# Attention accumulators laid out by head and query half in a four-layer attention kernel

## The chip, the cores and the metric

The kernel runs on one core of a Trainium2 chip. The metric is the device time of one execution in microseconds. The kernel before takes 5525.5 us (median of 3 runs, 5524.3 to 5525.83).

## The reference

Four layers follow one another on x of shape [1, 2048, 576]. Layers 0 and 2 are multi-head attention (32 heads of 18 channels, with keys and values of their own), layers 1 and 3 have one key and one value head for all 32 query heads. Everything is float32.

```python
x = x + _A_ref(_layernorm(x), A_wqkv, A_wo)
x = x + _B_ref(_layernorm(x), B_wq, B_wk, B_wv, B_wo)
x = x + _A_ref(_layernorm(x), A_wqkv, A_wo)
x = x + _B_ref(_layernorm(x), B_wq, B_wk, B_wv, B_wo)
# within a layer, per head:
scores = jnp.einsum("bhqd,bhkd->bhqk", q, k) * (Dh ** -0.5)
p = softmax(scores); o = jnp.einsum("bhqk,bhkd->bhqd", p, v)
```

## The kernel before, in words

A layer projects queries, keys and values, and then goes through 16 pairs of heads (index p), each in four quarters of 512 queries (index u). There are 64 such blocks a layer and 256 in all. For one block (p, u) three kinds of work run on TensorE (PE).

- Row maxima: 32 matmuls of 128 queries by 512 keys (`max_mm`, lines 639 and 653), each read by VectorE (DVE, lines 656 and 658), some of them first copied by ScalarE (ACT, line 651). They run 14 steps (`LEAD`) ahead of the exponentials.
- Scores and exponentials: 32 matmuls of 128 keys by 512 queries (`exp_mm`, line 879), each followed by one ACT instruction (line 883), which writes a tile `pt` of 128 x 512. Tile i belongs to head a = (i // 2) % 2 of the pair and to key chunk kc = i // 4 * 2 + i % 2, so that each head has 16 chunks of 128 keys.
- Values: `pv_block` (line 921) multiplies `pt` by the values with a column of ones beside them, 19 columns, into the PSUM bank `oacc`. A float32 matmul appears in the trace as two instructions and two weight loads.

`oacc` has four groups of 32 partitions. Before the change group j = 64a + 32(kc % 2) holds head a, summed over the even or over the odd key chunks, for all 512 queries. One block of `pv_block` takes two key chunks and both heads, that is four tiles `pt`, one in each group; the four groups run at the same time in four column strips of the array.

The order of the work on PE is written out by hand. `UNIT` is a list of ten units; each names its 4 to 7 score and maximum matmuls (called rows here), and how many columns of values follow them: 448, 480, 320, 256, 480, 448, 416, 416, 416, 416. Ten units make 4096 columns, which is one block (eight steps of 512). Values lag by `PV_LAG` = 928 columns, the first two units. `pv_cols` cuts a unit's columns at the borders of the accumulator's width, and each piece is four matmuls of one width. Rows take their PSUM bank from seven in turn, the oldest first, so a row waits until ACT or DVE has read what was there.

After a block's last piece, one instruction copies `oacc` away to a tile `oc`: ACT (line 930) while maxima are still to be done, otherwise DVE (two blocks a layer). GpSimd (POOL) then adds the two halves of the keys (`o_sum`: two copies and one addition into `sums[u % 2]`). The rest of the way goes through DRAM and is run by `run_todo` at due times counted in steps from the block's end: `l_part` (5) loads the row of sums of exponentials, `l_inv` (8) takes the reciprocal on POOL, `l_out` (8) and `l_rows` (11) store it and load it again spread over partitions into `rb`, `o_mul` (13) multiplies on POOL, and `o_out` (15) stores the result to `o_d`. All DMAs are issued by SyncE (SP) in program order, among them `max_rows`, which brings the maxima to the scores' operand two steps before they are used. `sums` has two buffers, one for even and one for odd quarters.

Of the kernel before, what the change touches and what calls it, by code (L numbers as in the profile page):

```python
# [8 lines left out]
F32 = mybir.dt.float32  # L9
F32R = mybir.dt.float32r  # L10
AF = mybir.ActivationFunctionType
OP = mybir.AluOpType
# [5 lines left out]
DH = D // H  # L18
P = 128
NCH = S // P  # L20
# [25 lines left out]
STEPS = 8  # L46
LEAD = 14
NM_AT = 2.5
ROW_AT = 5
SUM_AT = 3.75  # L50
L_AT = 5
INV_AT = 8
R_AT = 8
RB_AT = 11
# [32 lines left out]
def tile_kernel(ctx: ExitStack, tc: tile.TileContext, A_x, A_wqkv, A_wo, B_x, B_wq, B_wk, B_wv, B_wo, out):  # L87
    nc = tc.nc
# [3 lines left out]
    cst = ctx.enter_context(tc.tile_pool(name="cst", bufs=1))  # L92
# [32 lines left out]
    oacc = psum.tile([P, 512], F32, name="oacc")  # L125
# [16 lines left out]
    o_d = dram.tile([D, S], F32, name="o_d")  # L142
    r_d = dram.tile([H, S], F32, name="r_d")
    x_d = dram.tile([len(AWAY), P, D], F32, name="x_d")

    rb = cst.tile([P, 512], F32, name="rb")

    sums = [cst.tile([P, 512], F32, name=f"os{i}") for i in range(2)]

# [29 lines left out]
    def ptile(name, shape=(P, 512), dt=F32):  # L179
        return pool.tile(list(shape), dt, tag="p", bufs=15, name=name)  # L180

    def copy(eng, dst, src):
        if eng is nc.scalar:
            eng.activation(dst, src, AF.Copy)
        else:
            eng.tensor_scalar(dst, src, 1.0, 0.0, op0=OP.mult, op1=OP.add)  # L186
# [271 lines left out]
    for layer in range(4):  # L458
        is_a = layer % 2 == 0
# [6 lines left out]
        def v_of(c):  # L466
            return vs[c // 8][:, c % 8] if is_a else vs[0][:, c]
# [73 lines left out]
        def q_slot(p):  # L541
            return (3, 5, 1)[p % 3] if is_a else (3, 4, 0)[p % 3]
# [38 lines left out]
                    fixed_rows(k_slot(p), True)  # L581
                load_rows(k_slot(p), D + 2 * p * DH, DH, 0, S, (i - 2,))

        mxs, nms, pts, ocs = {}, {}, {}, {}

        def ops(p):
            return big[:, q_slot(p)], big[:, k_slot(p)]
# [11 lines left out]
        for a in range(2):  # L599
            n = -4 * LEAD % 32  # L600
# [6 lines left out]
            left = [(i // 2 % 4, i // 8 * 2 + i % 2) for i in range(16)]  # L607
            left = [x for x in left if x not in order]
# [11 lines left out]
        ns = STEPS * 4 * NPAIR  # L620
# [281 lines left out]
        turn, pv_at = [0], [0]  # L902

        def pv_cols(cols):

            while cols:
                n, c0 = divmod(pv_at[0], 512)
                w = min(cols, 512 - c0)
                pv_block(n, c0, c0 + w)
                pv_at[0] += w  # L910
                cols -= w

        def pv_block(n, c0, c1):

            p, u, i = *divmod(n // STEPS, 4), n % STEPS * 4
            cs = slice(c0, c1)
            turn[0] += 1
            for i in range(i, i + 4) if turn[0] % 2 else range(i + 3, i - 1, -1):
                a, kc = (i // 2) % 2, i // 4 * 2 + i % 2
                j = 64 * a + 32 * (kc % 2)  # L920
                nc.tensor.matmul(oacc[j:j + DH + 1, cs], v_of(kc)[:, 2 * p + a if is_a else 0, :], pts[p, u, i][:, cs],  # L921
                                 start=kc < 2 and c0 == 0, stop=kc >= 14 and c1 == 512)
                if c1 == 512:
                    pt = pts.pop((p, u, i))
                    free.extend(j for j, x in enumerate(ring) if x is pt)
            if c1 == 512 and i // 4 == STEPS - 1:
                oc = ocs[p, u] = ocs["tile"]
                ticks[0] += 1
                if m_done[0] < 4 * ns:
                    nc.scalar.activation(oc, oacc, AF.Copy)  # L930
                else:
                    copy(nc.vector, oc, oacc)


        def o_sum(p, u):
            oc = ocs.pop((p, u))
            t = sums[u % 2]
            for j in (0, 64):
                copy(nc.gpsimd, t[j:j + 32], oc[j + 32:j + 64])
            nc.gpsimd.tensor_tensor(t[:96], t[:96], oc[:96], op=OP.add)  # L940

        def l_part(p, u):
            lt = lts[p, u] = pool.tile([P, 8], F32, name="lt")
            for a in range(2):
                nc.sync.dma_start(lt[64 * a:64 * a + 64, :], sums[u % 2][64 * a + DH:64 * a + DH + 1, :])

        def l_inv(p, u):
            rl = rls[p, u] = pool.tile([P, 8], F32, name="rl")
# [5 lines left out]

        def l_rows(p, u):
            for a in range(2):
                nc.sync.dma_start(rb[64 * a:64 * a + DH, :],
                                  r_d[2 * p + a:2 * p + a + 1, u * 512:(u + 1) * 512].to_broadcast([DH, 512]))

        def o_mul(p, u):  # L960
            t = sums[u % 2]
            nc.gpsimd.tensor_tensor(t[:96], t[:96], rb[:96], op=OP.mult)  # L962

        def o_out(p, u):
            for a in range(2):
                c = (2 * p + a) * DH
                nc.sync.dma_start(o_d[c:c + DH, u * 512:(u + 1) * 512], sums[u % 2][64 * a:64 * a + DH, :])


        relu, raw = (pool.tile([P, 640], F32, tag="xh", bufs=2, name=n) for n in ("relu", "raw"))  # L970
# [3 lines left out]
        def at(b, f, *args):  # L974
            todo.setdefault(b, []).append((f, args))
# [12 lines left out]
        for p in range(NPAIR):  # L988
            for u in range(4):
                b = STEPS * (4 * p + u) + STEPS - 1  # L990
                if is_a or p or u:
                    at(b + NM_AT, max_store, p, u)
                    at(b + (SOON[2] if b == ns - 1 else ROW_AT), max_rows, p, u)
                soon = p == NPAIR - 1 and u == 0
                for d, f in ((SUM_AT, o_sum), (L_AT, l_part), (INV_AT, l_inv), (R_AT, l_out), (RB_AT, l_rows),
                             (SOON[0] if soon else MUL_AT, o_mul), (SOON[1] if soon else O_AT, o_out)):
                    at(b + LEAD + d, f, p, u)
            if p + 1 < NPAIR and is_a:
                for d, f in ((0, diff_in), (3, diff_split), (5, diff_out), (10 if p else 8, diff_rows)):
                    at(max(LEAD, 32 * p - 8) + d, f, p + 1)  # L1000
            if is_a and p in (0, 1):
                at(LEAD + 20 + 32 * p, load_rows, q_slot(p + 1), 2 * (p + 1) * DH, DH, 1536, S)
            if p + 1 < NPAIR:
                for i in range(4 if is_a else 2):
                    at(LEAD + 32 * (p - 1) + 1 + 8 * i if p else LEAD + 1 + 4 * i, load_part, p + 1, i)
# [12 lines left out]
        def run_todo(st):  # L1018
            for n in sorted(n for n in todo if n <= st):
                for f, args in todo.pop(n):  # L1020
                    f(*args)
# [11 lines left out]
            f(*args)  # L1033
        assert not weave["left"] and m_done[0] == 4 * LEAD
        e_next = [0, 0]
        ocs["tile"] = ptile("oc")

        def exp_next(a, rank=0):
            pu, kc = divmod(e_next[a], NCH)
            exp_mm(*divmod(pu, 4), kc // 2 * 4 + 2 * a + kc % 2, rank)  # L1040
            e_next[a] += 1

        phase = lagged = 0
        while m_done[0] < 4 * ns:
            rows, cols = UNIT[phase % len(UNIT)]
            run_todo(LEAD + sum(e_next) / 4)
            for kind, a, rank in rows:
                if kind == "e":
                    exp_next(a, rank)
                elif m_done[0] < 4 * ns:  # L1050
                    max_mm(oldest(rank))
            skip = min(cols, PV_LAG - lagged)
            lagged += skip
            pv_cols(cols - skip)
            phase += 1
# [4 lines left out]
        while sum(e_next) < 4 * ns:  # L1060
            run_todo(LEAD + sum(e_next) / 4)
            for _ in range(min(4, 4 * ns - sum(e_next))):
                exp_next(int(e_next[0] > e_next[1]), next(i for i, j in enumerate(lru) if j not in held))
            left, c = 4 * ns - sum(e_next), -pv_at[0] % (512 * STEPS)
            if left < 4 * STEPS and 0 < c <= 512:
                pv_cols(c)
                for _ in range(FIRST[0]):
                    next(first)
                pv_cols(512 - c)
            else:  # L1070
                if left // 4 == 1:
                    for _ in range(FIRST[1]):
                        next(first)
                pv_cols(512)
# [39 lines left out]
```

## Time and profile before

| | kernel before |
|---|---|
| median time | 5525.5 us |
| profiled execution, span | 5520.9 us (4.6 us below the median time) |
| PE busy | 5509.2 us (100%) |
| DVE busy | 4920.3 us (89%) |
| ACT busy | 4889.3 us (89%) |
| POOL busy | 1839.9 us (33%) |
| chain that ended last | PE 97%, of it line 921 38%, line 879 27%, line 653 17% |

Busy times of PE overlap, since matmuls in different strips of the array run together, and their ends are modelled; so PE's pace is read from the distance between starts and not from its busy share. The span has four stretches of about 1.1 ms in which the blocks follow one another, one for each layer, with projections between them.

### The profile page before, as it was taken

The numbers are of one execution on the slowest core, as the hardware profiler recorded it, in microseconds if no ns is written. First come the engines' busy times: TensorE is split into PE (matmuls) and PEld (weight loads), VectorE is DVE, ScalarE is ACT, GpSimd is POOL, SyncE is SP. The second block draws the span as 40 slices with busy tenths as digits, with TensorE's granted clock in tenths as the row PEclk, the third lists the DMA queues.
The fourth block names the chain that finished last, engine by engine and source line by source line (L and its number), as shares of the span: only waits on it lengthen the run. The fifth ranks groups of instructions, "written<-read, shape, count | busy, mean of one in ns | idle before, by whom it ended". The sixth has DMA issues, their size and how long they took to land.

```text
span 5520.9 us, 143086 instructions
## 1 busy us (share of the span) xinstructions
PE 5509.2 (100%) x55774; PEld 3050.7 (55%) x55774; DVE 4920.3 (89%) x9493; ACT 4889.3 (89%) x9882; POOL 1839.9 (33%) x2382
## 2 busy tenths in 40 slices
PE   9999999999999999999999999999999999999999
PEld 8655555454855555555686555545458545454546
DVE  4799999998799999999637999999977999999995
ACT  3599999999299999999626999999992999999996
POOL 3243333334233323233412433333342333333332
PEclk9999999999999999999999999999999999999999
DMA  6321111111411000001243211111114111010002
GB/s 219 119 60 45 45 45 48 43 45 34 136 57 31 24 24 21 24 21 25 64 176 109 58 49 43 45 46 48 40 43 133 54 28 25 24 25 21 24 15 84
DMA packets 277610, 306.04 MB, mean 55 GB/s; under 512 B 136434, under 2 KB 194378, under 8 KB 267642
## 3 DMA queue, kind: packets, MB, share of 16 engines
q1 hardware_dynamic: 276930, 296.89, 18.7%
q8 instruction: 437, 7.16, 0.5%
q14 instruction: 243, 1.99, 0.1%
HBM read 169.68 MB, written 123.13 MB: 53 GB/s over the span
## 4 chain that ended last, share of the span: by engine, by line
PE 97%; issue 1%; DVE 1%; ACT 1%; DMA 0%; POOL 0%; SPq 0%; POOLq 0%; ACTq 0%
PE oacc L921 38%; PE pse L879 27%; PE psm L653 17%; PE psn L275 7%; PE psq L481 5%; PE psm L639 3%; DVE mx L658 1%; ACT pt L883 1%; PE ps L261 0%; POOL ev L494 0%; DMA m_d<-tr 0%; DMA qk_d<-ev 0%; PE oacc L262 0%; DMA big<-m_d 0%; DMA big<-qk_d 0%
## 5 line engine op out<-in xcount | busy, mean ns | idle before, releaser
L883 ACT ACTIVATE pt<-pse 128x512 f32<-128x512 f32 x8192 | 4185.0, 612 | 10.1 <-PE pse L879 1.9
L658 DVE TENSOR_REDUCE mx<-psm 128x1 f32<-128x512 f32 x6208 | 3942.4, 684 | 88.6 <-PE psm L653 66.3
L879 PE MATMUL pse<-big 64*128 64x512 f32 x8192 | 2280.5, 432 | 0.5 <-DMA big<-m_d 0.5
L653 PE MATMUL psm<-big 62*128 62x512 f32 x7200 | 2158.9, 443 | 2.2 <-ACT evr L493 0.8
L879 PEld LDWEIGHTS pse<-big 64*128 64x128 f32 x8192 | 1174.4, 184 | 1064.2 <-ACT pt L883 758.2
L921 PE MATMUL oacc<-pt,vbuf 128*19 128x32 f32 (+11 forms) x26544 | 1728.2, 368 | 0.3 <-ACT oc L930 0.2
L653 PEld LDWEIGHTS psm<-big 62*128 62x128 f32 x7200 | 878.2, 184 | 204.3 <-DVE mx L658 75.9
L921 PEld LDWEIGHTS oacc<-pt,vbuf 128*19 128x19 f32 x26544 | 533.9, 98 | 819.9 <-issue 661.4
L186 POOL TENSOR_SCALAR hl<-neg 128x8 fp32r<-128x8 f32 x256 | 50.6, 198 | 2462.2 <-DVE neg L854 2462.2
L921 PE MATMUL oacc<-pt,vy 128*19 128x288 f32 (+3 forms) x8176 | 566.3, 383 | 0.0
L949 POOL TENSOR_TENSOR rl<-lt,mone 128x8 f32<-128x8 f32 x256 | 422.0, 1648 | 320.0 <-DMA lt<-os 318.1
L656 DVE CUSTOM_DVE_ANT_0 relu<-psm,relu 128x512 f32<-128x512 f32 x496 | 342.9, 691 | 76.3 <-ACT pt L883 50.9
L186 POOL TENSOR_SCALAR os<-oc 32x512 f32<-32x512 f32 x512 | 315.3, 616 | 102.4 <-DVE oc L186 50.6
L656 DVE CUSTOM_DVE_ANT_0 xo<-psm,xo 128x512 f32<-128x512 f32 x496 | 332.1, 670 | 15.5 <-ACT pt L883 1.6
L490 ACT ACTIVATE ev<-psq 128x512 fp32r<-128x512 f32 (+1 forms) x112 | 66.9, 597 | 311.5 <-PE psq L481 222.4
L940 POOL TENSOR_TENSOR os<-os,oc 96x512 f32<-96x512 f32 x256 | 330.6, 1291 | 21.4
L962 POOL TENSOR_TENSOR os<-os,rb 96x512 f32<-96x512 f32 x256 | 327.9, 1281 | 23.1 <-DMA rb<-r_d 23.1
L921 PEld LDWEIGHTS oacc<-pt,vy 128*19 128x19 f32 x8176 | 189.8, 98 | 242.0 <-issue 197.7
L651 ACT ACTIVATE xo<-psm 128x512 f32<-128x512 f32 x496 | 317.1, 639 | 0.0
L275 PE MATMUL psn<-wsm,xx 128*128 128x288 f32 x2240 | 310.4, 297 | 0.1
L275 PEld LDWEIGHTS psn<-wsm,xx 128*128 128x128 f32 x2240 | 299.0, 188 | 15.4 <-issue 13.1
L651 ACT ACTIVATE relu<-psm 128x512 f32<-128x512 f32 x496 | 303.6, 612 | 0.0
(102 smaller groups left out, 2781.3 us busy)
## 6 DMA issues: line engine op xcount, KB each, us to landing
big<-qk_d SPq DMA_DIRECT2D x172, 432.0 KB
qk_d<-ev SPq DMA_DIRECT2D x96, 512.0 KB
qk_d<-ev SPq DMA_DIRECT2D x120, 256.0 KB
rb<-r_d SPq DMA_DIRECT2D x512, 36.0 KB
o_d<-os SPq DMA_DIRECT2D x512, 36.0 KB
o<-o_d SPq DMA_DIRECT2D x56, 256.0 KB
xx<-qk_d SPq DMA_DIRECT2D x120, 72.0 KB
big<-m_d SPq DMA_DIRECT2D x512, 4.0 KB
```

The lines of the kernel that those rows point to most:

```text
L186: eng.tensor_scalar(dst, src, 1.0, 0.0, op0=OP.mult, op1=OP.add)
L275: nc.tensor.matmul(ps, lhs[:, xc, :], wsm[:, wc, h * 288:(h + 1) * 288], start=i == 0, stop=i == len(TERMS) - 1)
L651: nc.scalar.activation(t, ps, AF.Relu)
L653: nc.tensor.matmul(ps, q[b:b + KM, c0:c0 + P], k[b:b + KM, kb * 512:(kb + 1) * 512], start=True, stop=True)
L656: nc.vector.tensor_tensor_reduce(t, ps, t, 1.0, LOWEST, OP.add, OP.max, mx[:, r:r + 1])
L658: nc.vector.reduce_max(mx[:, r:r + 1], ps, axis=AX.X)
L879: nc.tensor.matmul(e, k[r:r + KE, kc * P:(kc + 1) * P], q[r:r + KE, u * 512:(u + 1) * 512], start=True, stop=True)
L883: nc.scalar.activation(pt, e, AF.Exp, scale=SCALE)
L921: nc.tensor.matmul(oacc[j:j + DH + 1, cs], v_of(kc)[:, 2 * p + a if is_a else 0, :], pts[p, u, i][:, cs], start=kc < 2 and c0 == 0, stop=k ...
L940: nc.gpsimd.tensor_tensor(t[:96], t[:96], oc[:96], op=OP.add)
L949: nc.gpsimd.tensor_tensor(rl, lts.pop((p, u)), mone, op=OP.pow)
L962: nc.gpsimd.tensor_tensor(t[:96], t[:96], rb[:96], op=OP.mult)
```

## The change

The accumulator becomes 256 columns wide. Group j = 64a + 32h now holds head a and half h of the block's 512 queries, summed over all 16 key chunks. One block of `pv_block` takes one key chunk: two tiles `pt`, each read in two halves of 256 columns. The copy out of PSUM goes straight to `sums[u % 2]`, 256 columns wide instead of 512, and `o_sum` with its tile `oc` is gone. `l_part` is one DMA instead of two, `l_rows` fills 64 partitions with 256 columns instead of 18 with 512, `o_mul` works on 128 x 256 instead of 96 x 512, and `o_out` is four DMAs instead of two. `UNIT`, `PV_LAG` and the due times of the other steps are as before.

```diff
-SUM_AT = 3.75
-    rb = cst.tile([P, 512], F32, name="rb")
+    rb = cst.tile([P, 256], F32, name="rb")
...
         def pv_cols(cols):
             while cols:
-                n, c0 = divmod(pv_at[0], 512)
-                w = min(cols, 512 - c0)
+                n, c0 = divmod(pv_at[0], 256)
+                w = min(cols, 256 - c0)
...
         def pv_block(n, c0, c1):
-            p, u, i = *divmod(n // STEPS, 4), n % STEPS * 4
-            cs = slice(c0, c1)
+            p, u, kc = *divmod(n // NCH, 4), n % NCH
             turn[0] += 1
-            for i in range(i, i + 4) if turn[0] % 2 else range(i + 3, i - 1, -1):
-                a, kc = (i // 2) % 2, i // 4 * 2 + i % 2
-                j = 64 * a + 32 * (kc % 2)
-                nc.tensor.matmul(oacc[j:j + DH + 1, cs], v_of(kc)[:, 2 * p + a if is_a else 0, :], pts[p, u, i][:, cs],
-                                 start=kc < 2 and c0 == 0, stop=kc >= 14 and c1 == 512)
-                if c1 == 512:
-                    pt = pts.pop((p, u, i))
+            tiles = [(p, u, kc // 2 * 4 + 2 * a + kc % 2) for a in range(2)]
+            groups = [(a, h) for a in range(2) for h in range(2)]
+            for a, h in groups if turn[0] % 2 else groups[::-1]:
+                j = 64 * a + 32 * h
+                nc.tensor.matmul(oacc[j:j + DH + 1, c0:c1], v_of(kc)[:, 2 * p + a if is_a else 0, :],
+                                 pts[tiles[a]][:, 256 * h + c0:256 * h + c1],
+                                 start=kc == 0 and c0 == 0, stop=kc == NCH - 1 and c1 == 256)
+            if c1 == 256:
+                for t in tiles:
+                    pt = pts.pop(t)
                     free.extend(j for j, x in enumerate(ring) if x is pt)
-            if c1 == 512 and i // 4 == STEPS - 1:
-                oc = ocs[p, u] = ocs["tile"]
+            if c1 == 256 and kc == NCH - 1:
                 ticks[0] += 1
                 if m_done[0] < 4 * ns:
-                    nc.scalar.activation(oc, oacc, AF.Copy)
+                    nc.scalar.activation(sums[u % 2][:, :256], oacc[:, :256], AF.Copy)
                 else:
-                    copy(nc.vector, oc, oacc)
+                    copy(nc.vector, sums[u % 2][:, :256], oacc[:, :256])
-        def o_sum(p, u):
-            oc = ocs.pop((p, u))
-            t = sums[u % 2]
-            for j in (0, 64):
-                copy(nc.gpsimd, t[j:j + 32], oc[j + 32:j + 64])
-            nc.gpsimd.tensor_tensor(t[:96], t[:96], oc[:96], op=OP.add)
...
             lt = lts[p, u] = pool.tile([P, 8], F32, name="lt")
-            for a in range(2):
-                nc.sync.dma_start(lt[64 * a:64 * a + 64, :], sums[u % 2][64 * a + DH:64 * a + DH + 1, :])
+            nc.sync.dma_start(lt, sums[u % 2][DH::32, :256])
...
             for a in range(2):
-                nc.sync.dma_start(rb[64 * a:64 * a + DH, :],
-                                  r_d[2 * p + a:2 * p + a + 1, u * 512:(u + 1) * 512].to_broadcast([DH, 512]))
+                src = r_d[2 * p + a, u * 512:(u + 1) * 512].rearrange("(h t) -> h t", h=2)
+                nc.sync.dma_start(rb[64 * a:64 * a + 64, :], src[:, None, :].to_broadcast([2, 32, 256]))
...
-            t = sums[u % 2]
-            nc.gpsimd.tensor_tensor(t[:96], t[:96], rb[:96], op=OP.mult)
+            t = sums[u % 2][:, :256]
+            nc.gpsimd.tensor_tensor(t, t, rb, op=OP.mult)
...
-                nc.sync.dma_start(o_d[c:c + DH, u * 512:(u + 1) * 512], sums[u % 2][64 * a:64 * a + DH, :])
+                for h in range(2):
+                    j, t0 = 64 * a + 32 * h, u * 512 + 256 * h
+                    nc.sync.dma_start(o_d[c:c + DH, t0:t0 + 256], sums[u % 2][j:j + DH, :256])
...
-            left, c = 4 * ns - sum(e_next), -pv_at[0] % (512 * STEPS)
+            left, c = 4 * ns - sum(e_next), -pv_at[0] % (256 * NCH)
```

## Rows read from the trace of the kernel before

**Rows 1.** Page: chain by engine; score matmuls; weight loads of the values (busy, mean, idle)

```profile
PE 97%; issue 1%; DVE 1%; ACT 1%; DMA 0%; POOL 0%; SPq 0%; POOLq 0%; ACTq 0%
...
L879 PE MATMUL pse<-big 64*128 64x512 f32 x8192 | 2280.5, 432 | 0.5 <-DMA big<-m_d 0.5
...
L921 PEld LDWEIGHTS oacc<-pt,vbuf 128*19 128x19 f32 x26544 | 533.9, 98 | 819.9 <-issue 661.4
```

**Rows 2.** Windows: busy us of PE, PEld, DVE, ACT, POOL, clock, in layer 0's blocks

```profile
340.00:1340.00 1000.00, 999.82 (x10875) 501.95 (x10871) 964.31 (x1851) 998.33 (x2012) 371.27 (x474) 1.00 0.17 43
```

**Rows 3.** Timeline of PE over one block (start us, us, engine, line, operation, tiles, count)

```profile
800.90 0.74 PE L921 MATMUL oacc<-pt,vbuf 128*19 128x320 f32 x8
801.56 0.50 PE L879 MATMUL pse<-big 64*128 64x512 f32 x2
...
802.25 0.63 PE L921 MATMUL oacc<-pt,vbuf 128*19 128x192 f32 x16
...
803.71 1.01 PE L921 MATMUL oacc<-pt,vbuf 128*19 128x448 f32 x16
804.64 0.49 PE L653 MATMUL psm<-big 62*128 62x512 f32 x1
...
805.76 0.95 PE L921 MATMUL oacc<-pt,vbuf 128*19 128x448 f32 x8
806.64 0.50 PE L879 MATMUL pse<-big 64*128 64x512 f32 x1
...
807.77 0.90 PE L921 MATMUL oacc<-pt,vbuf 128*19 128x32 f32 x16
808.60 0.50 PE L879 MATMUL pse<-big 64*128 64x512 f32 x1
...
815.64 0.95 PE L921 MATMUL oacc<-pt,vy 128*19 128x416 f32 x16
816.53 0.50 PE L653 MATMUL psm<-big 62*128 62x512 f32 x1
...
817.44 1.00 PE L921 MATMUL oacc<-pt,vy 128*19 128x480 f32 x8
818.37 0.50 PE L879 MATMUL pse<-big 64*128 64x512 f32 x1
...
819.28 0.73 PE L921 MATMUL oacc<-pt,vbuf 128*19 128x320 f32 x8
```

**Rows 4.** Timeline of ACT from the same block's beginning

```profile
800.19 0.60 ACT L930 ACTIVATE oc<-oacc 128x512 f32<-128x512 f32 x1
800.68 2.55 ACT L883 ACTIVATE pt<-pse 128x512 f32<-128x512 f32 x5
803.07 0.66 ACT L651 ACTIVATE xo<-psm 128x512 f32<-128x512 f32 x1
...
804.57 0.62 ACT L651 ACTIVATE relu<-psm 128x512 f32<-128x512 f32 x1
805.21 3.54 ACT L883 ACTIVATE pt<-pse 128x512 f32<-128x512 f32 x7
```

**Rows 5.** Timeline of PE, end of layer 0: rows without maxima

```profile
1354.97 0.73 PE L879 MATMUL pse<-big 64*128 64x512 f32 x4
1355.63 1.06 PE L921 MATMUL oacc<-pt,vbuf 128*19 128x192 f32 x16
```

**Rows 6.** Timeline of ACT, end of layer 0: an instruction of 256 columns

```profile
1382.37 0.42 ACT L184 ACTIVATE xx<-o 128x256 fp32r<-128x256 f32 x1 [0.37 <-DMA o<-o_d]
```

**Rows 7.** Timeline of POOL, one block: the halves of the keys

```profile
821.58 1.30 POOL L186 TENSOR_SCALAR os<-oc 32x512 f32<-32x512 f32 x2
822.97 1.28 POOL L940 TENSOR_TENSOR os<-os,oc 96x512 f32<-96x512 f32 x1
```

**Rows 8.** Timeline of SP, the same block: results out, maxima in

```profile
825.68 0.80 SPq L967 DMA_DIRECT2D o_d<-os  x2
826.59 0.52 SPq L868 DMA_DIRECT2D big<-m_d  x2
```

More of the change, by code (lines that the diff above doesn't have):

```diff
@@ L582, in load_part @@
                 load_rows(k_slot(p), D + 2 * p * DH, DH, 0, S, (i - 2,))
-        mxs, nms, pts, ocs = {}, {}, {}, {}
+        mxs, nms, pts = {}, {}, {}
         def ops(p):
@@ L994, in tile_kernel @@
                 soon = p == NPAIR - 1 and u == 0
-                for d, f in ((SUM_AT, o_sum), (L_AT, l_part), (INV_AT, l_inv), (R_AT, l_out), (RB_AT, l_rows),
+                for d, f in ((L_AT, l_part), (INV_AT, l_inv), (R_AT, l_out), (RB_AT, l_rows),
                              (SOON[0] if soon else MUL_AT, o_mul), (SOON[1] if soon else O_AT, o_out)):
@@ L1035, in tile_kernel @@
         e_next = [0, 0]
-        ocs["tile"] = ptile("oc")
         def exp_next(a, rank=0):
```

## The prediction

> **What bounds the kernel now.** First the chain that ended last: TensorE holds 97% of it, GpSimd and the DMAs next to nothing [rows 1]. So what is taken from GpSimd can't be read as time saved; it counts only where PE waited for it. Next the windows of one stage of blocks: in 1000 us PE was busy for 999.8, ScalarE for 998.3 and VectorE for 964.3, at full clock [rows 2]. PE and ScalarE are both nearly full there, and the busy shares can't tell which of the two sets the pace. The third view does: PE's timeline over one block, read by distances between starts [rows 3]. A block goes from 800.90 to 819.28, 18.38 us, and 248 such blocks (62 a layer) are 4.56 ms of the 5.52. Ten stretches of values alternate with ten of rows. From a stretch's start to the first row behind it, 320 columns take 0.66 us, 448 take 0.88 and 480 take 0.93 [rows 3]: 0.22 us for 128 more columns and 0.27 for 160 more, so about 1.67 ns a column, which is four cycles of the 2.4 GHz clock, and a fixed 0.13 us beside it. That is PE at its own pace, with no wait in it. The rows are close to theirs: four rows take 0.69 us (801.56 to 802.25) [rows 3], and at the end of the layer, where ScalarE is not yet behind, four take 0.66 (1354.97 to 1355.63) [rows 5]. So PE sets the pace, and ScalarE adds a few hundredths where a row has to wait for its bank.
>
> ScalarE's timeline shows the other side [rows 4]. Exponentials follow one another every 0.48 us (five from 800.68 to 803.07), but the copy to relu at 804.57 is followed only 0.64 us later: there ScalarE waited for PE's next score. It catches up with PE within two units of the copy out of `oacc`, so what it gains at the copy lasts until there and no further.
>
> **The pieces of the value matmuls.** The columns streamed stay the same: before, 8 x 512 x 4 matmuls for a block, after, 16 x 256 x 4, four strips at a time. What changes is the number of pieces. Borders of units lie at 320, 576, 1056, 1504, 1920, 2336, 2752, 3168, 3616 and 4096 columns of a block. With multiples of 512 they cut a block into 17 pieces, with multiples of 256 into 25. So there are 8 more joints in a block, each with four matmuls and their weights, two instructions each.
>
> A joint's price stands in the trace, since some stretches have one already. With one piece (320, 448, 480) the three take 2.47 us for 1248 columns; less 1.667 ns a column (2.08 us) 0.130 us a stretch are left. With two pieces (448 and 32, 32 and 384, 416 and 32; the row names the first width, and x16 tells that there are two) they take 0.93, 0.83 and 0.89, 2.65 us for 1344 columns; less 2.24 us 0.137 a stretch are left [rows 3]. A joint costs some 6 ns; hundredths of a microsecond round it, so its ends are 0 and 10 ns. It lies on PE's own stream, where nothing covers it: 8 x 6 = 48 ns a block, 12.3 us for 256 blocks (0 to 20.5).
>
> Most of the added joints look like the measured ones, with 32 to 256 columns on either side. New are stretches of three pieces (64, 256, 96 for instance), one more piece of 32 columns and two more of 64. A loading of the values' weights takes 98 ns [rows 1], as long as 59 columns; yet the piece of 32 columns, 53 ns, costs no more than the others, ahead of a long piece and behind one [rows 3]. So the loads run beside the matmuls of earlier pieces, and I take none of their time.
>
> Here a rule speaks against the change. The Trainium skill, "TensorEngine Tiling (Array Packing)", section "Instruction Overhead", says that a matmul carries about 60 cycles of overhead and that one with a single column takes as long as one with 60. By it a piece of 32 columns would take 28 columns' time too long, an estimated 47 ns for both its passes, and one more of them would add some 12 us to the sum. The trace disagrees: 32 and 384 columns together take 0.83 us, which is 0.137 over their stream, like the rest [rows 3].
>
> **The copy out of PSUM.** On ScalarE it takes 0.60 us for 512 columns [rows 4]; the nearest row with 256 columns takes 0.42 [rows 6]. So 0.18 us a block go from ScalarE, 248 x 0.18 = 45 us of its work. It may have to wait for more semaphores than before, which takes a little of this back. On the path only the rows gain that wait for ScalarE between the copy and the point at which it waits for PE again: the four rows at 801.56, which are 0.69 - 0.66 = 0.03 us over the same four without such waits [rows 3, 5], and perhaps a hundredth in the next unit. I take 0.03 us for 248 blocks, 7.4 us; the ends are 0 (VectorE holds the same rows) and 0.05 us, 12.4 us.
>
> **GpSimd's addition.** Its two copies (1.30 us) and the addition (1.28) go [rows 7], and `o_mul` gets narrower: well over 2.58 us a block, some 660 us of GpSimd's 1840. None is on the path. What GpSimd made earlier is waited for by DMAs whose due times stay. So I take nothing; if a due time were late because of GpSimd, it would be a gain at a layer's end only.
>
> **The new wait.** The copy now writes `sums`, which `o_out` of the block two before must have read. Behind the copy on ScalarE stand all later exponentials, and PE's rows wait for these. `o_out` for the block copied at 800.19 is issued at 825.68 and takes SyncE 0.80 us for two DMAs [rows 8]; four would be 1.6. The next copy into that buffer comes two blocks later, at 800.19 + 2 x 18.38 = 836.95. 9.7 us are left to land, so I cost the wait at nothing; without that cover each microsecond late would stop ScalarE for one. In SyncE's order `max_rows` stands behind `o_out` (826.59 [rows 8]); two more DMAs there, less one of `l_part`, delay it by at most 0.8 us, and `l_rows` with more rows to write may take as much again. It is due two steps, 4.6 us, ahead of its use, and PE waited for these rows for 0.5 us in the whole execution [rows 1]. So nothing, up to 2 us in all.
>
> **Layer ends.** In the last two blocks of a layer the joints count as well (in the 256 above), save where ScalarE sets the pace; VectorE's copy there is shorter, off the path.
>
> **The sum.** +12.3 - 7.4 = +4.9 us on the profiled 5520.9, and the same on the median of 5525.5, which lies 4.6 above it: 5530 us. With the ends of the terms it goes from -12.4 to +22.5, 5513 to 5548.
>
> **The rivals.**
> Joints without relief: VectorE's releases hold the same rows as ScalarE's, so the shorter copy moves nothing, and the joints cost 6 to 10 ns. That is 5538 to 5546, slower. It decides once the relief is under 0.005 us a block with a joint at 6 ns. For it: VectorE is 96% busy in the stage [rows 2]. Against: the four rows without maxima are 0.03 shorter [rows 3, 5]. Chance 0.22.
> ScalarE is the bound: all 0.18 us a block come off, 5525.5 - 45 = 5481, or with the joints 5493. For it: 998.3 us of 1000 busy [rows 2]. Against: 0.64 us where 0.48 would do [rows 4], a wait for PE. Chance 0.09.
> A narrow piece has a floor: when three pieces follow each other with 32 or 64 columns among them, their weights (98 ns) are late. One 32-wide piece held to 98 ns costs 45 ns more a block, 11.5 us, 5541; both passes of it and of the two 64-wide ones held to 98 ns (196 less 53, and twice 196 less 107) cost 321 ns, 82 us, 5612. For it: no stretch of three is in the trace. Against: the 32-wide pieces that are. The tiling page's 60 cycles come to the lower of these. Chance 0.07.
> The change moves nothing that counts, or a late `max_rows` or `sums` costs microseconds: 5524 to 5530, within the forecast; a wait of `sums` that shows in each block I give 0.02.
>
> **How the numbers follow.** The forecast, 5530 with 5518 to 5537 around it, has 0.60. A measurement of this kernel can tell about 0.2% (11 us) from no change, so faster is under 5514.5 and slower over 5536.5. The range of 8 in 10 takes in the first rival and the ends of the terms: 5513 to 5547. Faster: the second rival and a larger relief with free joints, 0.13. Slower: the first, the floor and the wait, 0.30. The same: 0.57.
>
> **What would show it.** In the profile after, a stretch of 416 columns in three pieces should take about 0.84 us where two took 0.83, and one of 480 in two pieces 0.94 where one took 0.93. A block should be 18.40 us, give or take 0.03. ScalarE's copy should stand at 0.42, the four rows behind it at 0.66 to 0.67, and ScalarE should wait for PE earlier than at 804.57. GpSimd's busy time should fall to about 1100 us with no change on the chain. I am wrong if a stretch of three pieces takes over 0.87 us, if the rows of units far from the copy change their length, or if the copy on ScalarE shows a wait for a DMA.

## The result and the profile after

The changed kernel takes 5531.86 us (median of 20 runs, 5529.39 to 5537.59), the kernel before in the same comparison 5524.38 us (20 runs). The ratio is 1.0014, with a 95% interval of 1.0008 to 1.0021: 7.5 us slower, 4.4 to 11.6 by the interval. The profiled execution has a span of 5529.7 us, 8.8 more than before.

The page of the changed kernel: busy times, the chain by engine, the largest group of weight loads.

```profile
span 5529.7 us, 176153 instructions
...
PE 5518.6 (100%) x72158; PEld 3504.0 (63%) x72158; DVE 4925.7 (89%) x9493; ACT 4867.9 (88%) x9882; POOL 1055.4 (19%) x1614
...
PE 97%; issue 1%; DVE 1%; POOL 0%; DMA 0%; ACT 0%; SPq 0%; POOLq 0%; ACTq 0%
...
L920 PEld LDWEIGHTS oacc<-pt,vbuf 128*19 128x19 f32 x38832 | 885.2, 98 | 923.0 <-issue 497.7
```

GpSimd lost 785 us of work and the chain is as in [rows 1]: still PE. PE has 16384 matmul instructions more, which is 256 blocks x 8 joints x 4 groups x 2. The same stage as in [rows 2] (columns: busy us of PE, PEld, DVE, ACT, POOL, clock) shows ScalarE with some room now, 991.9 us of 1000 instead of 998.3:

```profile
340.00:1340.00 1000.00, 999.92 (x14324) 596.67 (x14324) 965.20 (x1846) 991.88 (x2009) 204.73 (x310) 1.00 0.17 47
```

PE's timeline over one block, to be held against [rows 3] (start us, us; x16 has two pieces and x24 three, of which the first width is named):

```profile
803.35 0.74 PE L920 MATMUL oacc<-pt,vbuf 128*19 128x256 f32 x16
804.02 0.50 PE L878 MATMUL pse<-big 64*128 64x512 f32 x2
...
804.69 0.63 PE L920 MATMUL oacc<-pt,vbuf 128*19 128x192 f32 x16
...
806.17 1.01 PE L920 MATMUL oacc<-pt,vbuf 128*19 128x192 f32 x24
807.11 0.49 PE L652 MATMUL psm<-big 62*128 62x512 f32 x1
...
808.24 0.95 PE L920 MATMUL oacc<-pt,vbuf 128*19 128x224 f32 x16
809.12 0.50 PE L878 MATMUL pse<-big 64*128 64x512 f32 x1
...
810.29 0.91 PE L920 MATMUL oacc<-pt,vbuf 128*19 128x32 f32 x24
811.12 0.50 PE L878 MATMUL pse<-big 64*128 64x512 f32 x1
...
821.76 0.74 PE L920 MATMUL oacc<-pt,vbuf 128*19 128x256 f32 x16
```

This block lasts 18.41 us (803.35 to 821.76). Its first stretch of values has become 0.67 us (0.66), the third 0.94 (0.93); the four rows at 804.02 are down to 0.67 us from 0.69. And one thing that I had not expected: the seven rows behind the 448 columns take 1.17 us (809.12 to 810.29), where they took 1.13 in [rows 3] (806.64 to 807.77).

ScalarE's timeline from the copy on, against [rows 4]:

```profile
802.67 0.40 ACT L930 ACTIVATE os<-oacc 128x256 f32<-128x256 f32 x1
802.99 2.66 ACT L882 ACTIVATE pt<-pse 128x512 f32<-128x512 f32 x5
805.53 0.60 ACT L650 ACTIVATE xo<-psm 128x512 f32<-128x512 f32 x1
...
807.03 0.60 ACT L650 ACTIVATE relu<-psm 128x512 f32<-128x512 f32 x1
807.74 3.54 ACT L882 ACTIVATE pt<-pse 128x512 f32<-128x512 f32 x7
```

The copy went from 0.60 to 0.40 us. The five exponentials behind it take 2.54 us to the next start (2.39 before): ScalarE waits for PE among them, earlier than before, as forecast. But from the relu at 807.03 to the next exponential it is 0.71 us, where it was 0.64. That is the place from which the rows behind the 448 columns are late.

Distances between starts, taken over a whole trace, show differences that one block, read in hundredths of a microsecond, can't. The table has the ten stretches of a block in order, as means over the 248 blocks of each trace, in nanoseconds: columns of values, the time of the stretch of values, and the time of the rows behind it.

| columns | 320 | 256 | 480 | 448 | 416 | 416 | 416 | 416 | 448 | 480 | sum |
|---|---|---|---|---|---|---|---|---|---|---|---|
| values less 1.667 ns a column, before | 132 | 137 | 137 | 132 | 136 | 137 | 137 | 138 | 136 | 132 | |
| the same, after | 141 | 141 | 142 | 136 | 142 | 142 | 137 | 143 | 141 | 137 | |
| rows, before | 684 | 908 | 1126 | 1129 | 1130 | 1153 | 1131 | 1133 | 918 | 906 | 10218 |
| rows, after | 671 | 901 | 1127 | 1168 | 1127 | 1129 | 1132 | 1129 | 919 | 905 | 10209 |

The values grow by 48 ns a block, the rows shrink by 9. The mean block goes from 18398 to 18436 ns; 38 ns times 248 are 9.4 us, against 8.8 in the spans. Not all of the 48 ns are joints. By medians over the blocks the values grow by 41 ns: 5 ns in each of the eight stretches that got a joint, and 1 ns in the stretch of 256, which got none. Most of the other 7 ns comes from two single blocks, the first of layers 0 and 2, whose first two stretches together take almost 1 us longer after the change.

GpSimd's timeline at `o_mul` (start us, us, line, tiles), against [rows 7, 8]:

```profile
823.93 0.74 POOL L953 TENSOR_TENSOR os<-os,rb 128x256 f32<-128x256 f32 x1
```

The additions that stood here before are gone; the multiplication is left. SyncE's timeline at `o_out`, in the same columns:

```profile
809.15 1.51 SPq L960 DMA_DIRECT2D o_d<-os  x4
810.76 0.52 SPq L867 DMA_DIRECT2D big<-m_d  x2
```

The four DMAs of `o_out` take 1.51 us to issue and `max_rows` stands behind them. PE waited as little for it as before (its matmuls of the scores have 0.5 us of idle time in all, 0.3 of it for these rows).

### The profile page after: what moved, and what is told of

Read it like the earlier page. It is cut to its first block, busy times and chain, and to the rows that moved or that the text cites. A ratio compares the mean times of both kernels' runs of the same rounds, so it can differ in the third digit from the quotient of the medians.

```text
span 5529.7 us, 176153 instructions
## 1 busy us (share of the span) xinstructions
PE 5518.6 (100%) x72158; PEld 3504.0 (63%) x72158; DVE 4925.7 (89%) x9493; ACT 4867.9 (88%) x9882; POOL 1055.4 (19%) x1614
## 4 chain that ended last, share of the span: by engine, by line
PE 97%; issue 1%; DVE 1%; POOL 0%; DMA 0%; ACT 0%; SPq 0%; POOLq 0%; ACTq 0%
PE oacc L920 38%; PE pse L878 27%; PE psm L652 17%; PE psn L274 7%; PE psq L480 5%; PE psm L638 3%; PE ps L260 0%; DVE mx L657 0%; POOL ev L493 0%; DMA qk_d<-ev 0%; ACT pt L882 0%; DMA big<-qk_d 0%; PE oacc L261 0%; POOL big L214 0%; DMA xo<-in_A_x_dram 0%
## 5 line engine op out<-in xcount | busy, mean ns | idle before, releaser
L878 PE MATMUL pse<-big 64*128 64x512 f32 x8192 | 2280.4, 432 | 0.5 <-DMA big<-m_d 0.3
L652 PE MATMUL psm<-big 62*128 62x512 f32 x7200 | 2167.3, 443 | 1.6 <-ACT evr L492 0.7
L920 PE MATMUL oacc<-pt,vbuf 128*19 128x256 f32 (+7 forms) x38832 | 1738.0, 304 | 0.0
L878 PEld LDWEIGHTS pse<-big 64*128 64x128 f32 x8192 | 1177.0, 184 | 536.4 <-ACT pt L882 280.8
L920 PEld LDWEIGHTS oacc<-pt,vbuf 128*19 128x19 f32 x38832 | 885.2, 98 | 923.0 <-issue 497.7
L652 PEld LDWEIGHTS psm<-big 62*128 62x128 f32 x7200 | 895.6, 184 | 194.1 <-ACT pt L882 57.4
L920 PE MATMUL oacc<-pt,vy 128*19 128x256 f32 (+2 forms) x12272 | 568.7, 310 | 0.0
L920 PEld LDWEIGHTS oacc<-pt,vy 128*19 128x19 f32 x12272 | 296.1, 98 | 242.5 <-issue 127.4
L274 PEld LDWEIGHTS psn<-wsm,xx 128*128 128x128 f32 x2240 | 298.9, 188 | 11.7 <-issue 10.2
L495 DVE TENSOR_TENSOR ev<-psq,ev 128x512 fp32r<-128x512 f32 (+1 forms) x84 | 58.0, 691 | 205.6 <-ACT ev L489 192.3
L953 POOL TENSOR_TENSOR os<-os,rb 128x256 f32<-128x256 f32 x256 | 189.5, 740 | 136.4 <-DMA rb<-r_d 61.8
L638 PE MATMUL psm<-big 54*128 54x512 f32 x512 | 214.6, 419 | 0.0
```

Of the source, the lines that this page charges most:

```text
L274: nc.tensor.matmul(ps, lhs[:, xc, :], wsm[:, wc, h * 288:(h + 1) * 288], start=i == 0, stop=i == len(TERMS) - 1)
L638: nc.tensor.matmul(ps.rearrange("p (h t) -> p h t", h=2) if p == 0 or not is_a else ps, q[b:b + 3 * DH, c0:c0 + P], k, start=True, stop=True)
L652: nc.tensor.matmul(ps, q[b:b + KM, c0:c0 + P], k[b:b + KM, kb * 512:(kb + 1) * 512], start=True, stop=True)
L878: nc.tensor.matmul(e, k[r:r + KE, kc * P:(kc + 1) * P], q[r:r + KE, u * 512:(u + 1) * 512], start=True, stop=True)
L920: nc.tensor.matmul(oacc[j:j + DH + 1, c0:c1], v_of(kc)[:, 2 * p + a if is_a else 0, :], pts[tiles[a]][:, 256 * h + c0:256 * h + c1], start ...
L953: nc.gpsimd.tensor_tensor(t, t, rb, op=OP.mult)
```

## The experiments

Two runs ask what the loss is made of.

**The joints alone.** The kernel before, with its pieces cut at 256 too:

```diff
-                w = min(cols, 512 - c0)
+                w = min(cols, 256 - c0 % 256)
```

> The kernel before, with its pieces cut at multiples of 256 columns as well: 25 pieces a block instead of 17, and nothing else. Theory (a joint costs 5 to 6 ns on PE's stream, not covered): stretches of two pieces instead of one grow by 5 ns, a block from 18.38 to 18.42 us, the run by 10 us to 5535. Rival (the joints are hidden by the rows' waits for ScalarE and VectorE): 5525, no change.

Measured: 5536.32 us against 5525.77 of the kernel before on the same chip, ratio 1.0021 (1.0012 to 1.003), 10.5 us. The values grow by 48 ns a block in the mean and by 40 in medians, which is 5 ns for each of the 8 joints; 9 of the 48 come from two blocks, the first of layers 0 and 2. The rows grow by 4 together: the four behind the first stretch take 12 ns more, those behind the second 416 take 13 less. The joints are worth what was expected of them, and they are paid for on PE (40 ns times 256 are 10.2 us).

**The release of the tiles.** In the changed kernel a tile `pt` comes free after its own chunk. Here four come free together again:

```diff
-            if c1 == 256:
-                for t in tiles:
-                    pt = pts.pop(t)
+            if c1 == 256 and kc % 2:
+                for i in range(kc // 2 * 4, kc // 2 * 4 + 4):
+                    pt = pts.pop((p, u, i))
                     free.extend(j for j, x in enumerate(ring) if x is pt)
```

> The changed kernel, but the four tiles pt of a pair of key chunks are given back together at the end of the odd chunk instead of two by two. The program then has almost no exponential that waits for ScalarE's own earlier instruction (before: one a block, changed kernel: two). Theory (the finer release makes ScalarE wait for itself, about 60 ns at the first score of a unit, and PE's rows behind the 448 columns grow from 1.13 to 1.17 us): those rows return to about 1.13 us, a block takes 18.36 us and the run 5521 to 5524 us, no longer slower than before. Rival (all of the loss is the joints, the row lengths are chance): the block stays at 18.40 us and the run at 5531.

Measured: 5522.65 us against 5525.77, ratio 0.9994 (0.9985 to 1.0003). The loss is gone, though a block takes 18405 ns in the mean and not the 18.36 us expected. The seven rows behind the 448 columns take 1132 ns in the mean (1168 in the changed kernel); in the trace's timeline of PE they go from 807.18 to 808.32:

```profile
806.30 0.95 PE L920 MATMUL oacc<-pt,vbuf 128*19 128x224 f32 x16
807.18 0.50 PE L878 MATMUL pse<-big 64*128 64x512 f32 x1
...
808.32 0.91 PE L920 MATMUL oacc<-pt,vbuf 128*19 128x32 f32 x24
```

What differs at ScalarE is a count. No activation in these traces carries more than one wait; where two are needed, the other stands ahead of it as an instruction of its own (EVENT_SEMAPHORE). The views of the line of the exponentials list these beside the activations. Before:

```profile
L883 ACTq EVENT_SEMAPHORE  x354: 17/17/240, 207.3 to 5457.7; - x177
```

After:

```profile
L882 ACTq EVENT_SEMAPHORE  x590: 17/17/232, 207.1 to 5451.0; - x197
```

With the release in fours:

```profile
L882 ACTq EVENT_SEMAPHORE  x102: 17/17/245, 207.4 to 5443.7; - x102
```

Before, there is about one such wait a block, at the 26th exponential behind the copy. After, there are two in almost every block, at the 8th, which is the one behind that relu, and at the 30th, shortly ahead of the next copy. At each of these ScalarE waits for PE and for an earlier instruction of its own (the former user of the tile it is given). By the program the latter is long done, since PE has read the tile in between, so what should cost time is the instruction ahead and not the earlier work; no run separates the two. The activation starts 62 ns (median) after the wait's 17 ns instruction does. By its place the wait at the 8th hits the first score of a unit, for which ScalarE has nothing else to do. From the relu to this exponential it is 641 ns before, 695 after and 641 with the release in fours (medians).

**Another choice, the release as changed.** To tell the wait from the time of the release:

```diff
-                j = old[0] if old and not by_act else max(free, key=lambda j: wrote[j])
+                j = old[0] if old else max(free, key=lambda j: wrote[j])
```

> The changed kernel with its fine release, but another choice among the free tiles pt: one whose last write PE has already seen is taken whenever there is one, and not only where VectorE read the bank last. By the program the exponential that waits for ScalarE's own instruction at the first score behind the 480 columns (the tenth after the copy) is gone, and one just ahead of the next copy stays. Theory (that wait, and not the time of the release, made the rows behind the 448 columns longer): they go from 1.17 to 1.13 us, a block from 18.44 to 18.40 us in the mean, the run to 5522 to 5526. Rival (the release in pairs itself is what helped in e1_release): the rows stay at 1.17 us and the run at 5532.

Measured: 5523.07 us against 5525.86, ratio 0.9997 (0.9988 to 1.0006). The rows behind the 448 columns are at 1132 ns and a block at 18400 in the mean.

```profile
L882 ACTq EVENT_SEMAPHORE  x350: 17/17/248, 207.1 to 5442.1; - x175
```

ScalarE's timeline from the relu to the 8th exponential, to be held against the 0.71 us of the changed kernel:

```profile
805.89 0.61 ACT L650 ACTIVATE relu<-psm 128x512 f32<-128x512 f32 x1
806.55 3.55 ACT L882 ACTIVATE pt<-pse 128x512 f32<-128x512 f32 x7
```

It is 0.66 us here (640 ns in the median of all blocks). Tiles come free as early as in the changed kernel, so the time of the release is not the cause. Both of the changed kernel's waits are gone; one for PE alone has come at the 31st exponential, the loss is gone with them, and there are about as many waits as in the kernel before. No run takes away one of the two waits alone. That the one behind the relu counts follows from its place: of the rows, those behind the 448 columns give back 37 ns, and the four behind the next copy only 3.

Three runs take the shorter copy apart.

**The long copy back.**

```diff
-                    nc.scalar.activation(sums[u % 2][:, :256], oacc[:, :256], AF.Copy)
+                    nc.scalar.activation(sums[u % 2], oacc, AF.Copy)
```

> The changed kernel, but ScalarE copies all 512 columns of the bank, of which the second half is not used. Theory (the shorter copy relieves the four rows behind the first stretch by 0.02 us and little else): those rows return from 0.66 to 0.68 us and the run is 4 to 6 us slower than the changed kernel, 5536. Rival (the shorter copy moves nothing on the path): 5531, as the changed kernel. Rival (ScalarE sets the pace): 0.18 us a block, 45 us slower, 5576.

Measured: 5549.01 us against 5525.77, ratio 1.0042 (1.0028 to 1.0055), some 17 us over the changed kernel's 5531.86 and more than the 4 to 6 expected. Most of the loss is in one place: the four rows behind the first stretch, 729 ns in the mean against 671 in the changed kernel (57 of the 68 ns that a block grows by). One of them (806.22 to 806.95):

```profile
806.22 0.51 PE L878 MATMUL pse<-big 64*128 64x512 f32 x2
...
806.95 0.63 PE L920 MATMUL oacc<-pt,vbuf 128*19 128x192 f32 x16
```

**The same without ScalarE's waits for itself**, that is e1_release with the diff above.

> As e1_release, but ScalarE copies 512 columns again. In e3_copy512 the longer copy cost 0.068 us a block, more than the 0.02 expected. Theory (the copy is worth more there because ScalarE, late by its waits for itself, had no time left; without these waits it is worth what the kernel before shows, 0.02 us): 5 us over e1_release, 5528, and the four rows behind the first stretch at 0.69 us. Rival (0.068 us whatever else): 17 us over e1_release, 5540, those rows at 0.73.

Measured: 5532.79 us against 5526.31, ratio 1.0012 (1.0003 to 1.0021). That is 10 us over e1_release by the medians; a block is 30 ns longer in the mean, the four rows take 694 ns instead of 667. So the cost lies between the theory's 5 us and the rival's 17. The copy is worth less where ScalarE doesn't come late to it, as the theory says, if more than I gave it. That ScalarE comes late in the changed kernel stands in the traces: there the copy starts 478 ns after the exponential ahead of it (median), which is ScalarE's own pace, and with the short copy in e1_release 522 ns, so that ScalarE still waits.

**The short copy alone**, in the kernel before:

```diff
-                    nc.scalar.activation(oc, oacc, AF.Copy)
+                    nc.scalar.activation(oc[:, :256], oacc[:, :256], AF.Copy)
...
+        nc.gpsimd.memset(ocs["tile"], 1.0)
```

> The kernel before, but ScalarE copies only the first 256 of the 512 columns of oacc (the results of the other half are left out). The shorter copy alone. Theory: the four rows behind the first stretch go from 0.684 to 0.667 us and the six behind the second by a hundredth, 0.02 to 0.03 us a block, 5 to 7 us under the kernel before, 5519. Rival (0.068 us a block): 17 us, 5508. Rival (VectorE holds the same rows): 5525.

Measured: 5519.18 us against 5526.31, ratio 0.9986 (0.9978 to 0.9995), 7.1 us. That is 2.8 to 12 us by the interval. The four rows go from 684 to 673 ns, and the rows of a block get 19 ns shorter together. Half of the results are left out here, so this is no kernel to use.

**GpSimd's addition back**, on a scratch tile:

```diff
+        def o_sum(p, u):
+            t, oc = sums[u % 2], scr[0]
+            for j in (0, 64):
+                copy(nc.gpsimd, oc[j:j + 32], t[j + 32:j + 64])
+            nc.gpsimd.tensor_tensor(oc[:96], oc[:96], t[:96], op=OP.add)
...
+                for d, f in ((3.75, o_sum), (L_AT, l_part), (INV_AT, l_inv), (R_AT, l_out), (RB_AT, l_rows),
...
+        scr = [ptile("scr")]
+        nc.gpsimd.memset(scr[0], 0.0)
```

> The changed kernel, with GpSimd's two copies and its addition put back at their old due time, on a scratch tile that nobody reads. Theory (GpSimd is off the path): GpSimd's busy time rises by about 650 us and the run stays within 3 us of the changed kernel, 5531. Rival (GpSimd's work disturbs VectorE or SyncE's queue, so that its removal is worth microseconds): slower by 5 us or more, 5536.

Measured: 5532.76 us against 5525.77, ratio 1.0012 (1.0003 to 1.0021), where the changed kernel has 1.0014. GpSimd is busy for 1703.8 us instead of 1055.4, and the block is the same to 4 ns. The addition cost nothing and its removal gave nothing.

**More joints.**

```diff
-                w = min(cols, 256 - c0)
+                w = min(cols, 128 - c0 % 128)
```

> The changed kernel with its pieces cut at multiples of 128 columns as well: 40 pieces a block instead of 25. Theory (5 ns a joint, weights load beside the matmuls): 75 ns a block, 18 us more than the changed kernel, 5550. Rival (narrow pieces have a floor, their weights of 98 ns are late): stretches grow by 16 ns or more a joint, 60 us and more, over 5590.

Measured: 5545.59 us against 5526.31, ratio 1.0033 (1.0021 to 1.0045). The values of a block grow by 75 ns over the changed kernel's, 5.0 for each of the 15 joints; the rows give 19 back, and the run is some 14 us over the changed kernel by the medians and not 18. No floor appears, even in stretches of five pieces with 32 and 64 columns among them.

**Borders moved onto the joints.** As e1_release, with the columns of `UNIT` set to 416, 512, 256, 256, 512, 512, 384, 384, 448, 416.

> As e1_release, with the units' columns changed so that seven of their ten borders fall on multiples of 256: 416, 512, 256, 256, 512, 512, 384, 384, 448, 416. A block has 19 pieces instead of 25. Theory (a joint is 5 ns and the rows keep their lengths): 30 ns a block less than e1_release, 7 us, 5515. Rival (units of uneven length make rows wait for ScalarE and VectorE): rows get longer by more than 30 ns a block and the run is at 5522 or above.

Measured: 5572.32 us against 5526.31, ratio 1.008 (1.0068 to 1.0093). A miss, 57 us over the forecast and 50 over e1_release. The values are 26 ns shorter than in e1_release, since six joints are gone, but the rows of a block are 220 ns longer. Behind the first of the stretches of 384 columns the rows take 1.18 us or more (817.05 to 818.24 in one block) where they took 1.13 behind 416:

```profile
816.27 0.85 PE L920 MATMUL oacc<-pt,vbuf 128*19 128x256 f32 x16
817.05 0.50 PE L878 MATMUL pse<-big 64*128 64x512 f32 x1
...
818.24 0.42 PE L920 MATMUL oacc<-pt,vbuf 128*19 128x128 f32 x8
```

32 columns less are 53 ns less for PE, and the rows behind get 46 and 68 ns longer (means of the two stretches of 384). The rows behind the second stretch of 256 and behind the 448 that became 416 get 47 and 57 ns longer. In the views of the rows' two main lines (L878 and L652), the idle time of PE's weight loads that ScalarE ended goes from 309 us in e1_release to 575, and what VectorE ended from 59 to 389. So in these units ScalarE and VectorE set the length, and 32 columns more elsewhere give nothing back. PE sets the pace only while the units are cut so that the three come out even.

No version here that computes the whole result beats both kernels beyond the measurement: e1_release and e10_choice are 9 us under the changed kernel and, by their intervals, not to be told from the kernel before.

## Why the prediction was right, and where not

The forecast was 5530 us, 4.9 above before, with no change beyond the measurement as the likeliest outcome; it came to 5531.86, 7.5 above.

- What bounds: right. PE's own stream paces the blocks; the addition put back on GpSimd moves nothing (e4_pool), and ScalarE's 0.18 us a block did not come off.
- The joints: right in place and nearly in size. I read 6 ns from hundredths; the whole traces give 5, or 40 ns a block. That the values grew by 48 ns in the mean, the number in the sum, is chance, since two single blocks make up most of the difference. Alone the joints cost 10.5 us (forecast 12.3), and at 40 pieces they are still 5.0 ns (e2_joints, e6_cut128). A joint is two more matmuls in each strip; the Trainium skill, "TensorE: Matmul & The Clock Gate", section "Wait — 56ns, not 53.3ns?", gives a fixed 2.5 ns for each matmul at full clock, which would be an estimated 5 ns. The traces agree, with 5.0 ns.
- The shorter copy: right in place, the size is not one number. I took 30 ns a block; the four and six rows behind the copy gained 20, in the kernel before the short copy alone brings 7.1 us (forecast 7.4), and in the changed kernel taking it back costs 17 us. A row that waits pays only what lies beyond PE's own pace, so the price depends on how late ScalarE comes to the copy.
- GpSimd's addition and the new wait on `sums`: right, nothing. The copy of the changed kernel starts 478 ns after the exponential ahead of it in the median, at ScalarE's own pace.
- What failed is a step that I left out. I wrote that rows far from the copy would show me wrong, and they do: those behind the 448 columns grew by 39 ns, a fifth of a per cent of a block, and those behind the second 416 shrank by 24. The first is the earlier release of `pt`, which the prediction does not mention and so put at nothing: it changed which tile an exponential gets, and with it where a second wait stands ahead of an exponential (e1_release, e10_choice: both go back to 1132 ns). The second comes with the joints for the greater part (1140 ns in e2_joints, 1139 in e1_release, 1153 before); the rest goes with the added waits, since the changed kernel, e3_copy512 and e6_cut128 have about 1130 and the two runs without the waits 1137 to 1139. So these rows give back some 9 of the 39 ns. Why joints make them shorter stays open.
- That the sum came out is in part luck. In the mean of a block it is +48 for values, -20 for the copy, +39 and -24 for these rows, -5 elsewhere, together +38 ns (the forecast had +48 and -30). What was left out is +39, and most of it was cancelled by the -24 and -5 that were left out as well.
- The rivals: joints without relief is refuted by e9_before_copy256, ScalarE as the bound by the changed kernel itself, a floor for narrow pieces by e6_cut128, down to pieces of 32 columns, whose two passes stream for 27 ns each; no narrower piece was run. The e5_borders run shows that ScalarE and VectorE lie so close behind PE that a unit shortened by 32 columns is theirs.

## What to carry to other kernels

Before joining work in another grain, count what the new grain does to instruction boundaries on the engine that sets the pace; here each cost 5 ns, and the work taken from an idle engine paid for none of it. When buffers come free at other times, compare for each instruction on the second-busiest engine which buffer it gets and what it waits for: one more wait in the wrong place cost about as much as all the added joints (39 ns a block in its rows, against 40). Where engines are balanced by hand, price a saving by the row that waits for it and not by the instruction that got shorter.

## What was not expected of the hardware

An activation on ScalarE that needs two waits, one of them for ScalarE itself, starts 62 ns after the wait that is put ahead of it when ScalarE has nothing else to do, though the wait's own instruction shows only 17 ns. Pieces of 32 columns, 53 ns long, lose nothing beyond the joint, though the load of their weights is shown with 98 ns; in stretches of five pieces a joint is still 5.0 ns.
